# Attention outputs of one unit and scores of the next issued as one run of small matmuls, with masked scores and decayed keys and queries kept in the unit's own tile, and a new hand-written order for the first chunk

## Chip, cores and metric

The kernel runs on one core of one Trainium2 chip. Its time is the device time of one execution in microseconds (us); the figure that counts is the median over runs. The engines that matter are TensorE (PE; its weight loads are listed as PEld), VectorE (DVE), ScalarE (ACT), and the SyncE queue (SP), which issues nearly all DMA transfers. Each engine works through its own instructions in order; semaphores tie the engines together.

## The reference

Two layers, one after the other, in 32-bit floats, for 4 batches, 8 heads, 768 positions and a head width of 64. First an attention with decay, in blocks of 64 positions:

```python
for b in range(nb):                       # 12 blocks of 64 positions
    intra = (q_b @ k_b^T) * Dmask         # scores inside the block, masked by powers of lam
    intra = intra @ v_b
    inter = (q_b * lam_pow) @ kv_state    # what earlier blocks left
    out_b = intra + inter
    kv_state = lam_block * kv_state + (k_b * rev_pow)^T @ v_b
```

Its output, as 3072 tokens by 512 features, goes through a feed-forward layer: `h = x @ w_in` (512 by 2048), `g = softplus(h)`, `out = g @ w_out` (2048 by 512).

## The kernel before

The 768 positions are six **chunks** of 128 (two blocks of 64 each). A **unit** g is one chunk and one pair of heads: 24 units, four per chunk, `g // 4` being the chunk. A unit's inputs lie in one tile `att`: q and k with features on the partitions, k and v again with positions on the partitions.

The feed-forward layer runs in 96 **steps** s, 16 per chunk (one for each 128 columns of `w_in`). `mlp1(s)` (line 351) is 12 matmuls of 128x512 into a PSUM bank h; `chain_act`, `chain_hi`, `chain_lo` (lines 339 to 349) turn h into softplus values g, split into a high and a low part; `mlp2([s - 4])` (line 365) is 12 matmuls into four accumulators o. Both operands are split into high and low parts, hence three matmuls per product. The weights are converted and split on the chip, in groups of two, by `scale` and `round` (ACT), `shift`, `sign`, `add` (DVE), `hi` (ACT) and `lo` (DVE), lines 207 to 235; this goes on until about step 16.

The attention of units 4 to 23 is done by these functions:

- `k_decay` (line 262, ACT) and `q_decay` (line 268, DVE) write decayed copies kd and qd into tiles of their own, of tag b2.
- `mm_scores` (line 275) is one run of 64x64 matmuls: the scores into the x half and the state's increments into the y half of a tile w. That tile comes from `work` (tag t, one buffer of two PSUM banks).
- `mask_scores` (line 301, DVE) writes the masked scores into another b2 tile, and `update_states` (line 315, DVE) computes the next states from y with four instructions.
- `mm_out` (line 288) is a second run of 64x64 matmuls, from states, qd, values and masked scores, into a tile z, also from `work`. `x_high` (ACT) and `x_low` (DVE) then split z into the x that `mlp1` reads.

In the record, a 64x64 product is two matmul instructions, so `mm_scores` and `mm_out` show 64 instructions each.

Chunk 0 (units 0 to 3) uses 128-wide versions of the same (S, m, O, Q and so on). Steps 0 to 5 are an order written out by hand as a text (line 485): each entry names a function and its numbers, for example `mlp 1 2` for p = 2 of `mlp1(1)`. `warm n` issues n matmuls of zeros that nobody reads; 16 of them run before the text (line 151). From step 6 on a loop (line 509) emits the work. The scores of a unit stand behind `mlp2` of one step, and its outputs behind `mlp2` of the step two later:

```python
    scores_at.update({4 * n + 1 + NF: 2 * NP + n for n in range(NG - 2 * NP)})
    outs_at = {6: 4, **{s + 2: g for s, g in scores_at.items()}}
```

The PSUM banks are: o with four buffers (also used in chunk 0), h with two, and the two banks of `work`. A tile of a tag takes a bank whose earlier tile has been released at that place of the program, and its first writer waits until the last reader of that earlier tile is done. SBUF tiles of tag b8 (21 buffers) hold units, raw and split weights, x and the output rows.

Of the kernel before, what the change touches and what calls it, by code (L numbers as in the profile page):

```python
# [31 lines left out]
def decay_attention_softplus_ffn(  # L32
# [197 lines left out]
    def w_hi(*ks):  # L230
        nc.scalar.copy(out=w_at(ks)[:, 0], in_=conv[ks[0]].bitcast(F32))  # L231

    def w_lo(*ks):
        w = w_at(ks)
        nc.vector.tensor_sub(out=w[:, 1], in0=conv.pop(ks[0]).bitcast(F32), in1=w[:, 0])  # L235
# [38 lines left out]

    def mm_scores(g, x, y):
        q, k, kd, v = q_of(g), k_of(g), kds.pop(g), vt_of(g)
        for b in range(B):
            for t in range(2):
                cols = slice((2 * b + t) * 64, (2 * b + t + 1) * 64)
                for s in range(2):  # L280
                    r = half(s)
                    nc.tensor.matmul(x[r, cols], lhsT=k[r, b, t], rhs=q[r, b, t], start=True, stop=True)  # L282
                    if s == 0 or not last_chunk(g):
                        nc.tensor.matmul(  # L284
                            y[half(1 - s), cols], lhsT=kd[r, b, t], rhs=v[r, b, t], start=True, stop=True
                        )

    def mm_out(g, w):
        a, qd, v, st = aa.pop(g), qds.pop(g), vt_of(g), states[g]
        for b in range(B):  # L290
            cols = slice(b * 64, b * 64 + 64)
            for s in range(2):
                r = half(s)
                for t in range(2):
                    nc.tensor.matmul(w[half(t), s, cols], lhsT=st[r, b, t], rhs=qd[r, b, t], start=True, stop=False)  # L295
            for s in range(2):
                r = half(s)
                for t in range(2):
                    nc.tensor.matmul(w[half(t), s, cols], lhsT=v[r, b, t], rhs=a[r, b, t], start=False, stop=True)  # L299

    def mask_scores(g, x):
        a = aa[g] = t2([128, B, 2, 64], F32, f"a_{g}")
        m = mask[:, heads(g), :].rearrange("q (o t) i -> q o t i", o=1).broadcast_to([128, B, 2, T])
        nc.vector.tensor_mul(out=a, in0=x.rearrange("q (b t i) -> q b t i", b=B, t=2), in1=m)  # L304
# [85 lines left out]
    def scores_of(g):  # L390
        w = work(f"w{g}")
        mm_scores(g, w[:, 0], w[:, 1])
        mask_scores(g, w[:, 0])
        update_states(g, w[:, 1])
# [80 lines left out]
    step = {  # L475
        "S": scores0, "m": mask0_scores, "O": out0, "xh": x0_high, "xl": x0_low, "kd": k0_decay, "kda": k0_decay_act,
        "Q": sums0, "sc": states0, "kd1": k_decay, "qd": q_decay, "sc1": scores1,
        "m1": lambda g: mask_scores(g, z[g][:, 0]), "up": lambda g: update_states(g, z[g][:, 1]), "out1": out1,
        "xh1": lambda g: x_high(g, z[g]), "xl1": lambda g: x_low(g, z[g]),
        "scale": w_scale, "round": w_round, "shift": w_shift, "sign": w_sign,  # L480
        "add": w_add, "hi": w_hi, "lo": w_lo, "act": chain_act, "ghi": chain_hi, "glo": chain_lo,
# [1 line left out]
        "warm": keep_warm, "load": w_load, "unit": load_upto, "qk": loads["qk"], "v": loads["v"], "kt": loads["kt"],  # L483
    }
    for line in """
        S 0, m 0 0, scale 0, m 0 1, round 0, warm 6, S 1, shift 0, sign 0, add 0, scale 1, m 1 0, m 1 1,
        shift 1, warm 3, O 0, hi 0, lo 0, round 1, xh 0, sign 1, S 2, xl 0, scale 2, mlp 0 0, add 1, m 2 0,
        hi 1, O 1, load 4, xh 1, v 2, kt 0, m 2 1, shift 2, round 2, lo 1, xl 1, S 3, v 3, kda 2, mlp 1 0, m
        3 1, m 3 0, load 5, scale 3, shift 3, kda 0, round 3, mlp 1 1, O 2, O 3, xh 2, Q 0, sign 2, load 6,
        sign 3, xh 3, mlp 0 1, load 7, add 2, add 3, xl 2, mlp 0 2, xl 3, load 8, scale 4, kt 1, shift 4,  # L490
        scale 5, mlp 1 2, mlp 0 3, shift 5, hi 2, lo 2, hi 3, sign 5, round 5, round 4, mlp 1 3, mlp 2 0,
        load 9, act 0, scale 6 7, lo 3, sign 4, add 5, ghi 0, add 4, mlp 2 1, kda 1, hi 4, mlp 3 0, hi 5,
        round 6 7, mlp 3 1, shift 6 7, glo 0, kt 3, mlp 2 2, lo 4, act 1, mlp 3 2, load 10, lo 5, sign 6 7,
        unit 5, scale 8 9, kd 3, mlp 2 3, add 6 7, ghi 1, mlp 3 3, kd1 4, unit 6, mlp 4, Q 1, Q 2, sc1 4, hi
        6 7, load 11, Q 3, glo 1, shift 8 9, lo 6 7, qd 4, mlp 5, act 2, sc 1, ghi 2, load 12, sign 8 9, sc
        0, sc 3, glo 2, sc 2, load 13, load 14, round 8 9, m1 4, act 3, ghi 3, unit 7, mlp2 0, up 4, scale
        10 11, add 8 9, glo 3, hi 8 9, shift 10 11, mlp2 1, load 15, act 4, lo 8 9, load 16, ghi 4, round 10
        11, sign 10 11, glo 4, add 10 11
    """.replace("\n", " ").split(","):
# [4 lines left out]
    scores_at = {7: 5, 10: 6, 13: 7}
    scores_at.update({4 * n + 1 + NF: 2 * NP + n for n in range(NG - 2 * NP)})
    outs_at = {6: 4, **{s + 2: g for s, g in scores_at.items()}}
    for s in range(6, last + LAG):
        if s + 1 in scores_at:  # L510
            k_decay(scores_at[s + 1])
            q_decay(scores_at[s + 1])
# [4 lines left out]
        old, new = w_group(s - 1), w_group(s)
        if old:
            w_hi(*old)
        if new:  # L520
            w_scale(*new)
            w_round(*new)
        if old:
            w_lo(*old)
        if new:
            w_shift(*new)
            w_sign(*new)
            w_add(*new)
# [4 lines left out]
        if s in scores_at:  # L533
            scores_of(scores_at[s])
        if s in outs_at:
            g = outs_at[s]
            w = work(f"z{g}")
            mm_out(g, w)
            x_high(g, w)
            x_low(g, w)  # L540
        if s < last:
            mlp1(s)
        w_load(2 * s + 6)
        ahead = scores_at if s < 13 else outs_at
        if s in ahead:
            load_upto(ahead[s] + 2)
# [37 lines left out]
```

## Time and profile before

| | |
|---|---|
| median of 3 runs | 603.29 us (602.88 to 603.33) |
| profiled execution | 603.04 us |
| its span, first to last instruction | 601.3 us |
| instructions in the span | 11190 |
| matmul instructions of PE | 5017 |
| matmuls of `mlp1` and of `mlp2` | 1152 and 1152 |
| bytes read from and written to memory | 41.95 MB and 6.29 MB |

The profile is of one execution. In the list of instructions in order of time, the columns are start in us, duration in us, engine, line of the kernel, operation, tiles written and read, shapes, and the count of merged instructions; in square brackets stands the idle time of the engine before them and what ended it. The end of a matmul is modelled, so lengths of stretches of PE work are best taken from start to start. In the table of windows the columns are the window, its length, and busy time and instruction count of each engine, then the granted TensorE clock (1.00 is full speed), the share of the DMA engines and their rate.

### The profile page before, as it was taken

The numbers are of one execution on the slowest core, as the hardware profiler recorded it, in microseconds if no ns is written. First come the engines' busy times: TensorE is split into PE (matmuls) and PEld (weight loads), VectorE is DVE, ScalarE is ACT, GpSimd is POOL, SyncE is SP. The second block draws the span as 40 slices with busy tenths as digits, with TensorE's granted clock in tenths as the row PEclk, the third lists the DMA queues.
The fourth block names the chain that finished last, engine by engine and source line by source line (L and its number), as shares of the span: only waits on it lengthen the run. The fifth ranks groups of instructions, "written<-read, shape, count | busy, mean of one in ns | idle before, by whom it ended". The sixth has DMA issues, their size and how long they took to land.

```text
span 601.3 us, 11190 instructions
## 1 busy us (share of the span) xinstructions
PE 595.7 (99%) x5017; PEld 486.0 (81%) x5017; DVE 226.3 (38%) x337; ACT 211.4 (35%) x343; POOL 1.5 (0%) x9
## 2 busy tenths in 40 slices
PE   9999999999999999999999999999999999999997
PEld 6788888888888888888888888888888888888885
DVE  7999999623223133331332322312322121211011
ACT  5897867422322223222222232222322222222211
POOL 1000000000000000000000000000000000000000
PEclk9999999999999999999999999999999999999999
DMA  8997322223002206002023200220500200100001
GB/s 291 416 416 280 138 72 71 71 101 111 1 2 71 71 1 211 1 1 71 1 71 132 79 1 6 68 71 0 211 1 1 71 0 1 71 0 1 1 1 70
DMA packets 15743, 48.95 MB, mean 81 GB/s; under 512 B 1872, under 2 KB 1872, under 8 KB 15696
## 3 DMA queue, kind: packets, MB, share of 16 engines
q1 hardware_dynamic: 15408, 47.72, 21.8%
q8 instruction: 39, 0.64, 0.5%
q10 hardware_dynamic: 288, 0.52, 0.2%
q14 instruction: 8, 0.07, 0.0%
HBM read 41.95 MB, written 6.29 MB: 80 GB/s over the span
## 4 chain that ended last, share of the span: by engine, by line
PE 98%; DVE 1%; issue 0%; ACT 0%; DVEq 0%
PE h L360 45%; PE o L377 43%; PE w L282 3%; PE z L295 2%; PE z L299 2%; PE warm_ps L149 1%; PE w L284 1%; PE z L426 0%; PE x L410 0%; PE y L455 0%; DVE att L416 0%; DVE x L436 0%; DVE c L222 0%; ACT x L432 0%; DVE c L218 0%
## 5 line engine op out<-in xcount | busy, mean ns | idle before, releaser
L360 PE MATMUL h<-x,w 128*128 128x512 f32 x1152 | 282.8, 394 | 0.3 <-DVE x L436 0.3
L377 PE MATMUL o<-w,g 128*128 128x512 f32 x1152 | 275.9, 389 | 0.0
L377 PEld LDWEIGHTS o<-w,g 128*128 128x128 f32 x1152 | 216.3, 188 | 44.8
L360 PEld LDWEIGHTS h<-x,w 128*128 128x128 f32 x1152 | 212.9, 188 | 46.8 <-DVE x L436 1.2
L349 DVE TENSOR_TENSOR g<-l,g 128x512 fp32r<-128x512 f32 x96 | 66.4, 692 | 262.4 <-ACT g L345 262.3
L341 ACT ACTIVATE l<-h 128x512 f32<-128x512 f32 x96 | 57.2, 596 | 264.6 <-PE h L360 259.6
L345 ACT CAST g<-l 128x512 fp32r<-128x512 f32 x96 | 59.6, 621 | 2.9
L266 ACT ACTIVATE kd<-att,rp 128x256 f32<-128x256 f32 x40 | 18.2, 505 | 60.7 <-DMA att<-in_att 60.7
L309 DVE SCALAR_TENSOR_TENSOR st<-st,lam_c,w 64x256 f32<-64x256 f32 x72 | 31.7, 480 | 0.8
L271 DVE TENSOR_TENSOR qd<-att,lp 128x512 f32<-128x512 f32 x20 | 13.8, 689 | 34.7 <-DMA att<-in_att 34.7
L332 DVE TENSOR_TENSOR x<-z,x 128x512 fp32r<-128x512 f32 x20 | 13.8, 690 | 34.0 <-ACT x L325 34.0
L282 PEld LDWEIGHTS w<-att 64*64 64x64 f32 x640 | 20.4, 134 | 6.8 <-issue 6.0
L325 ACT CAST x<-z 128x512 fp32r<-128x512 f32 x20 | 11.7, 586 | 35.9 <-PE z L299 35.9
L282 PE MATMUL w<-att 64*64 64x64 f32 x640 | 23.1, 221 | 0.0
L284 PE MATMUL w<-att,kd 64*64 64x64 f32 x576 | 23.0, 221 | 0.0
L304 DVE TENSOR_TENSOR a<-w,mask 128x512 f32<-128x512 f32 x20 | 13.8, 690 | 24.3 <-PE w L284 18.3
L295 PEld LDWEIGHTS z<-qd,st 64*64 64x64 f32 x640 | 17.0, 134 | 7.0 <-issue 7.0
L295 PE MATMUL z<-qd,st 64*64 64x64 f32 x640 | 20.9, 224 | 0.0
L235 DVE TENSOR_TENSOR w<-c,w 128x1024 fp32r<-128x1024 f32 (+1 forms) x19 | 20.0, 1055 | 1.5 <-ACT w L231 1.5
L228 DVE CUSTOM_DVE_ANT_0 c<-raw,c 128x2048 uint16<-128x2048 uint16 (+1 forms) x19 | 19.9, 1056 | 1.5
L284 PEld LDWEIGHTS w<-att,kd 64*64 64x64 f32 x576 | 20.3, 134 | 0.0
L222 DVE SCALAR_TENSOR_TENSOR c<-raw,c 128x1024 uint32<-128x1024 uint32 (+1 forms) x19 | 20.0, 1055 | 0.4
(42 smaller groups left out, 182.4 us busy)
## 6 DMA issues: line engine op xcount, KB each, us to landing
att<-in_att SPq DMA_DIRECT2D x44, 512.0 KB, 5.1
raw<-in_wts SPq DMA_DIRECT2D x32, 512.0 KB, 8.5
out_dram<-ob SPq DMA_DIRECT2D x22, 256.0 KB, 2.6
att<-in_att SPq DMA_DIRECT2D x8, 256.0 KB, 8.3
out_dram<-ob ACTq DMA_DIRECT2D x2, 256.0 KB, 2.0
lam_b<-in_lam SPq DMA_DIRECT2D x1, 4.0 KB, 2.7
```

What stands on the lines that cost most here:

```text
L222: nc.vector.scalar_tensor_tensor(out=c, in0=raw_at(ks, 1), scalar=0x80000000, in1=c, op0=ALU.bitwise_and, op1=ALU.bitwise_or)
L228: nc.vector.tensor_add(out=c, in0=c, in1=raw_at(ks, 0))
L235: nc.vector.tensor_sub(out=w[:, 1], in0=conv.pop(ks[0]).bitcast(F32), in1=w[:, 0])
L282: nc.tensor.matmul(x[r, cols], lhsT=k[r, b, t], rhs=q[r, b, t], start=True, stop=True)
L284: nc.tensor.matmul(y[half(1 - s), cols], lhsT=kd[r, b, t], rhs=v[r, b, t], start=True, stop=True)
L295: nc.tensor.matmul(w[half(t), s, cols], lhsT=st[r, b, t], rhs=qd[r, b, t], start=True, stop=False)
L309: nc.vector.scalar_tensor_tensor(out=to[:, :, t], in0=of[:, :, t], scalar=lam_c[r, h : h + 1], in1=u[:, :, t], op0=ALU.mult, op1=ALU.add,)
L341: nc.scalar.activation(l_tiles[s], h_tiles.pop(s), AF.Softplus)
L345: nc.scalar.copy(out=g_tiles[s][:, 0, :], in_=l_tiles[s])
L349: nc.vector.tensor_sub(out=g[:, 1, :], in0=l_tiles.pop(s), in1=g[:, 0, :])
L360: nc.tensor.matmul(h_tiles[s], lhsT=w[:, i, cs], rhs=x[:, j, :], start=p == 0 and n == 0, stop=p == NP - 1 and n == 2,)
L377: nc.tensor.matmul(o_tiles[c][b], lhsT=g[:, i, b * 128 : (b + 1) * 128], rhs=w[:, j], start=f == 0 and n == 0, stop=f == NF - 1 and n == 2,)
```

## The change

**Tiles.** The tag b2 is gone. `k_decay` writes over k (position-major), `q_decay` over q, and `mask_scores` over k (feature-major), all in the unit's own tile. b8 gets a 22nd buffer. `mm_scores` and `mm_out` read from these places.

**Banks.** From unit 5 on, scores and increments go into two tiles of tag h, x and y, instead of a `work` tile. `mlp1`'s own h tiles take turns with them in the same two banks.

**Order in the loop.** An event every four steps holds `out1` (`mm_out`) of unit g - 1 and, right behind it, `sc1` (`mm_scores`) of unit g. One `mlp2` is pulled ahead from the following step to stand between them and `mlp1(s)`. The loop starts at step 17.

**The text.** It now reaches to step 16, with new places for most entries, and the order of the first loads is new. The decay of k of unit 2 moves from ACT (`kda`) to DVE (`kd`), and there are four `warm` matmuls in the text in place of nine.

```diff
-        return sb.tile(shape, dt, tag="b8", bufs=21, name=name)
+        return sb.tile(shape, dt, tag="b8", bufs=22, name=name)
...
-    for line in "w 1, qk 1, w 2, v 1, v 0, qk 2, w 3, qk 3, kt 2".split(","):
+    for line in "w 1, qk 1, w 2, v 0, qk 2, v 1, w 3, qk 3, v 2".split(","):
...
-            nc.scalar.activation(kd[:, :, t], kt_of(g)[:, :, t], AF.Copy, scale=rp1[:, h : h + 1])
+            nc.scalar.activation(kt_of(g)[:, :, t], kt_of(g)[:, :, t], AF.Copy, scale=rp1[:, h : h + 1])
...
+        q = q_of(g).rearrange("q b t i -> q b (t i)")
+        nc.vector.tensor_mul(out=q, in0=q, in1=w)
...
-        nc.vector.tensor_mul(out=a, in0=x.rearrange("q (b t i) -> q b t i", b=B, t=2), in1=m)
+        nc.vector.tensor_mul(out=k_of(g), in0=x.rearrange("q (b t i) -> q b t i", b=B, t=2), in1=m)
...
     def scores1(g):
-        z[g] = work(f"w{g}")
-        mm_scores(g, z[g][:, 0], z[g][:, 1])
+        if g == NP:
+            w = work(f"w{g}")
+            xy[g] = w[:, 0], w[:, 1]
+        else:
+            xy[g] = bank(f"x{g}"), bank(f"y{g}")
+        mm_scores(g, *xy[g])
...
+        S 0, m 0 1, scale 0, shift 0, sign 0, round 0, m 0 0, add 0, warm 3, S 1, scale 1, warm 1, O 0, m 1
+        0, hi 0, round 1, xh 0, shift 1, lo 0, sign 1, xl 0, kt 0, m 1 1, kt 1, v 3, round 2, S 2, scale 2,
+        load 4, add 1, m 2 0, mlp 0 0, hi 1, load 5, m 2 1, lo 1, O 1, S 3, xh 1, shift 2, load 6, load 7,
+        xl 1, kda 0, m 3 1, mlp 1 0, kda 1, m 3 0, sign 2, add 2, scale 3, mlp 1 1, load 8, O 2, xh 2, shift
+        3, xl 2, round 3, hi 2, load 9, O 3, sign 3, lo 2, unit 5, xh 3, kt 2, scale 4, load 10, Q 0, Q 1,
+        add 3, scale 5, shift 4, xl 3, hi 3, mlp 1 2, round 5, shift 5, mlp 0 1, sign 4, mlp 2 0, round 4,
+        scale 6 7, kt 3, mlp 0 2, mlp 2 1, mlp 0 3, act 0, sc 0, lo 3, ghi 0, unit 6, sign 5, add 4, shift 6
+        7, load 11, mlp 1 3, mlp 3 0, add 5, hi 4, hi 5, sign 6 7, mlp 3 1, round 6 7, glo 0, mlp 3 2, lo 5,
+        act 1, add 6 7, kd1 4, kd 2, mlp 2 2, ghi 1, mlp 3 3, hi 6 7, glo 1, mlp 2 3, load 12, act 2, mlp 4,
+        lo 4, Q 2, kd 3, scale 8 9, ghi 2, lo 6 7, shift 8 9, glo 2, sign 8 9, sc 1, sc1 4, Q 3, up 4, load
+        13, sc 2, act 3, mlp 5, sc 3, round 8 9, load 14, scale 10 11, add 8 9, ghi 3, shift 10 11, glo 3,
...
+        12 13, ghi 5, add 12 13, scale 14 15, qd 4, load 18, hi 12 13, mlp 6, glo 5, shift 14 15, mlp2 2,
+        mlp2 3, out1 4, load 19, lo 12 13, load 20, act 6, round 14 15, sign 14 15, load 21, ghi 6, load 22,
+        sc1 5, m1 5, add 14 15, load 23, mlp2 4, round 16 17, xh1 4, scale 18 19, scale 16 17, up 5, hi 14
...
+    events = {s: 2 * NP + (s - NF) // 4 for s in range(NF, last - NF + 1, 4)}
+    ahead = 17 - LAG
+    for s in range(17, last + LAG):
+        if events.get(s + 1, NG) < NG:
+            run("kd1", events[s + 1])
...
-        elif s - LAG < last - 1:
+        elif s - LAG < last - 1 and ahead != s - LAG:
             mlp2([s - LAG])
...
+        if s in events:
+            g = events[s]
+            run("out1", g - 1)
+            if g < NG:
+                run("sc1", g)
+            run("xh1", g - 1)
+            if g < NG:
+                run("m1", g)
+            if s % NF == 0:
+                run("xl1", g - 1)
+            if g < NG:
+                run("up", g)
+            if s % NF:
+                run("xl1", g - 1)
+            if g < NG:
+                run("qd", g)
+            ahead = s - LAG + 1
+            mlp2([ahead])
+            load_upto(g + 2)
         if s < last:
             mlp1(s)
```

More of the change, by code (lines that the diff above doesn't have):

```diff
@@ L48, in t8 @@
     def t8(shape, dt, name):
-        return sb.tile(shape, dt, tag="b8", bufs=21, name=name)
+        return sb.tile(shape, dt, tag="b8", bufs=22, name=name)
     def t4(shape, dt, name):
         return sb.tile(shape, dt, tag="b4", bufs=7, name=name)
-    def t2(shape, dt, name):
-        return sb.tile(shape, dt, tag="b2", bufs=4, name=name)
     def tl(shape, dt, name):
@@ L250, in x_of @@
         return x_tiles[c, p // 2][:, :, p % 2]
-    aa, kds, qds, states = {}, {}, {}, {}
+    states = {}
     lo, hi = half(0), half(1)
@@ L262, in k_decay @@
     def k_decay(g):
-        kd = kds[g] = t2([128, B, 2, 64], F32, f"kd_{g}")
         for t in range(2):
             h = heads(g).start + t
-            nc.scalar.activation(kd[:, :, t], kt_of(g)[:, :, t], AF.Copy, scale=rp1[:, h : h + 1])
+            nc.scalar.activation(kt_of(g)[:, :, t], kt_of(g)[:, :, t], AF.Copy, scale=rp1[:, h : h + 1])
     def q_decay(g):
-        qd = qds[g] = t2([128, B, 2, 64], F32, f"qd_{g}")
         w = lp[:, heads(g), :].rearrange("q (o t) i -> q o (t i)", o=1).broadcast_to([128, B, 2 * T])
-        nc.vector.tensor_mul(
-            out=qd.rearrange("q b t i -> q b (t i)"), in0=q_of(g).rearrange("q b t i -> q b (t i)"), in1=w
-        )
+        q = q_of(g).rearrange("q b t i -> q b (t i)")
+        nc.vector.tensor_mul(out=q, in0=q, in1=w)
     def mm_scores(g, x, y):
-        q, k, kd, v = q_of(g), k_of(g), kds.pop(g), vt_of(g)
+        q, k, kd, v = q_of(g), k_of(g), kt_of(g), vt_of(g)
         for b in range(B):
@@ L288, in mm_out @@
     def mm_out(g, w):
-        a, qd, v, st = aa.pop(g), qds.pop(g), vt_of(g), states[g]
+        a, qd, v, st = k_of(g), q_of(g), vt_of(g), states[g]
         for b in range(B):
@@ L388, in w_group @@
         return (2 * j, 2 * j + 1) if 2 * j < NW else ()
[L390 to L394, printed above, removed]
     def whole(p, kind):
@@ L465, in states0 @@
             )
+    xy = {}
     def scores1(g):
-        z[g] = work(f"w{g}")
-        mm_scores(g, z[g][:, 0], z[g][:, 1])
+        if g == NP:
[4 more added lines that the diff above has]
+        mm_scores(g, *xy[g])
     def out1(g):
@@ L485, in decay_attention_softplus_ffn @@
     for line in """
[L486 to L495, printed above, removed]
@@ L496, in decay_attention_softplus_ffn @@
-        0, sc 3, glo 2, sc 2, load 13, load 14, round 8 9, m1 4, act 3, ghi 3, unit 7, mlp2 0, up 4, scale
-        10 11, add 8 9, glo 3, hi 8 9, shift 10 11, mlp2 1, load 15, act 4, lo 8 9, load 16, ghi 4, round 10
-        11, sign 10 11, glo 4, add 10 11
+        S 0, m 0 1, scale 0, shift 0, sign 0, round 0, m 0 0, add 0, warm 3, S 1, scale 1, warm 1, O 0, m 1
+        0, hi 0, round 1, xh 0, shift 1, lo 0, sign 1, xl 0, kt 0, m 1 1, kt 1, v 3, round 2, S 2, scale 2,
+        load 4, add 1, m 2 0, mlp 0 0, hi 1, load 5, m 2 1, lo 1, O 1, S 3, xh 1, shift 2, load 6, load 7,
@@ new lines, in decay_attention_softplus_ffn @@
+        act 1, add 6 7, kd1 4, kd 2, mlp 2 2, ghi 1, mlp 3 3, hi 6 7, glo 1, mlp 2 3, load 12, act 2, mlp 4,
+        lo 4, Q 2, kd 3, scale 8 9, ghi 2, lo 6 7, shift 8 9, glo 2, sign 8 9, sc 1, sc1 4, Q 3, up 4, load
+        13, sc 2, act 3, mlp 5, sc 3, round 8 9, load 14, scale 10 11, add 8 9, ghi 3, shift 10 11, glo 3,
+        mlp2 0, load 15, hi 8 9, load 16, round 10 11, lo 8 9, sign 10 11, m1 4, act 4, mlp2 1, round 12 13,
+        load 17, ghi 4, add 10 11, scale 12 13, glo 4, shift 12 13, hi 10 11, kd1 5, lo 10 11, act 5, sign
@@ new lines, in decay_attention_softplus_ffn @@
+        12 13, ghi 5, add 12 13, scale 14 15, qd 4, load 18, hi 12 13, mlp 6, glo 5, shift 14 15, mlp2 2,
+        mlp2 3, out1 4, load 19, lo 12 13, load 20, act 6, round 14 15, sign 14 15, load 21, ghi 6, load 22,
+        sc1 5, m1 5, add 14 15, load 23, mlp2 4, round 16 17, xh1 4, scale 18 19, scale 16 17, up 5, hi 14
+        15, shift 18 19, lo 14 15, mlp 7, load 24, shift 16 17, mlp 8, load 25, unit 7, glo 6, scale 20 21,
+        sign 16 17, load 26, act 7, mlp2 5, round 18 19, kd1 6, load 27, add 16 17, hi 16 17, ghi 7, mlp 9,
@@ new lines, in decay_attention_softplus_ffn @@
+        qd 5, sign 18 19, lo 16 17, round 20 21, glo 7, add 18 19, unit 8, scale 24 25, load 28, load 29,
+        act 8, mlp2 6, xl1 4, ghi 8, glo 8, hi 18 19, out1 5, shift 20 21, act 9, lo 18 19, sc1 6, ghi 9,
+        round 22 23, kd1 7, scale 22 23, sign 20 21, mlp2 7, m1 6, add 20 21, mlp 10, shift 22 23, up 6,
+        load 30, hi 20 21, shift 24 25, glo 9, scale 28 29, mlp 11, act 10, lo 20 21, ghi 10, mlp2 8, round
+        24 25, unit 9, qd 6, glo 10, sign 22 23, act 11, ghi 11, xh1 5, add 22 23, hi 22 23, xl1 5, load 31,
@@ new lines, in decay_attention_softplus_ffn @@
+        glo 11, mlp 12, lo 22 23, sign 24 25, add 24 25, act 12, out1 6, sc1 7, m1 7, scale 26 27, shift 26
+        27, ghi 12, round 28 29, hi 24 25, glo 12, kd1 8, sign 26 27, lo 24 25, mlp2 9, xh1 6, shift 28 29,
+        mlp 13, load 32, round 26 27, act 13, add 26 27, scale 30 31, sign 28 29, hi 26 27, add 28 29, lo 26
+        27, xl1 6, mlp2 10, mlp 14, hi 28 29, ghi 13, glo 13, round 30 31, mlp2 11, shift 30 31, act 14, qd
+        7, ghi 14, glo 14, up 7, mlp 15, lo 28 29, act 15, sign 30 31, out1 7, ghi 15, sc1 8, up 8, add 30
@@ L499, in decay_attention_softplus_ffn @@
+        31, mlp2 12, mlp2 13, m1 8, xh1 7, unit 10, xl1 7, hi 30 31, mlp 16, lo 30 31, qd 8, glo 15
     """.replace("\n", " ").split(","):
@@ L501, in decay_attention_softplus_ffn, with run @@
         step[name](*map(int, numbers))
+    def run(name, *numbers):
+        step[name](*numbers)
     last = NCH * NF
[L506 to L512, printed above, removed]
+    events = {s: 2 * NP + (s - NF) // 4 for s in range(NF, last - NF + 1, 4)}
[3 more added lines that the diff above has]
+            run("kd1", events[s + 1])
         if s - 1 < last:
@@ L516, in decay_attention_softplus_ffn @@
             chain_lo(s - 1)
[L517 to L528, printed above, removed]
         if s == last + LAG - 2:
             mlp2([s - LAG, s - LAG + 1])
-        elif s - LAG < last - 1:
+        elif s - LAG < last - 1 and ahead != s - LAG:
             mlp2([s - LAG])
[L533 to L540, printed above, removed]
+        if s in events:
[17 more added lines that the diff above has]
+            load_upto(g + 2)
         if s < last:
             mlp1(s)
[L543 to L546, printed above, removed]
 def _layout(q, k, v, lam, w_in, w_out):
```

3 lines of the change are left out of this document (1 added, 2 removed).

## The prediction, made before the changed kernel had run

> **What bounds the kernel now.** I read the page's busy line first, then the slices of DVE, then the chain of work that ended last.
>
> ```profile
> PE 595.7 (99%) x5017; PEld 486.0 (81%) x5017; DVE 226.3 (38%) x337; ACT 211.4 (35%) x343; POOL 1.5 (0%) x9
> DVE  7999999623223133331332322312322121211011
> PE 98%; DVE 1%; issue 0%; ACT 0%; DVEq 0%
> ```
>
> TensorE is busy for 99% of the span and makes 98% of the chain, so only what shortens TensorE's own queue can shorten the kernel. The second row has a warning: from the second to the seventh of 40 slices (15 to 105 us, while weights are converted) VectorE is at 90% or more, so there a shorter TensorE queue helps only as far as VectorE keeps up.
>
> How TensorE spends its time is seen in the list in order of time, from start to start:
>
> ```profile
> 54.93 0.27 PE L282 MATMUL w<-att 64*64 64x64 f32 x1
> ...
> 56.02 3.02 PE L360 MATMUL h<-x,w 128*128 128x512 f32 x12
> 58.88 2.88 PE L377 MATMUL o<-w,g 128*128 128x512 f32 x12
> 61.60 2.88 PE L360 MATMUL h<-x,w 128*128 128x512 f32 x12
> 64.32 2.88 PE L377 MATMUL o<-w,g 128*128 128x512 f32 x12
> 67.13 0.34 PE L295 MATMUL z<-qd,st 64*64 64x64 f32 x8
> ...
> 67.41 0.30 PE L295 MATMUL z<-qd,st 64*64 64x64 f32 x8
> ...
> 67.88 0.30 PE L295 MATMUL z<-qd,st 64*64 64x64 f32 x8
> ...
> 68.22 3.02 PE L360 MATMUL h<-x,w 128*128 128x512 f32 x12
> 71.08 2.88 PE L377 MATMUL o<-w,g 128*128 128x512 f32 x12
> ```
>
> Twelve large matmuls in the middle of a stretch take 61.60 - 58.88 = 2.72 us, 0.227 each. The outputs of a unit start 67.13 - 64.32 = 2.81 after the twelve before them (0.09 late), run for 68.22 - 67.13 = 1.09, and the twelve behind them take 71.08 - 68.22 = 2.86 (0.14 late). One run of 64 small instructions thus costs 0.09 + 1.09 + 0.14 = 1.32 us. Inside it, 32 instructions pass in 67.88 - 67.41 = 0.47, so 64 take 0.94 of pure work. The rest, 1.32 - 0.94 = **0.38 us, is the price of going into small matmuls and out again**. The scores' run has the same figures: 56.02 - 54.93 = 1.09, then 2.86.
>
> **The change, part by part.**
>
> *The joined runs.* Units 4 to 23 have 20 runs of scores and 20 of outputs. Afterwards the outputs of units 4 to 22 stand right in front of the scores of units 5 to 23, with nothing for TensorE between them, in the text as in the loop: 19 entries and exits go. The number of small and large matmuls stays. Is the seam between the two free? Two places of chunk 0 bear on it:
>
> ```profile
> 16.06 1.09 PE L426 MATMUL z<-att 128*64 128x128 f32 x16
> 17.08 1.16 PE L410 MATMUL x<-att 64*128 64x128 f32 x16
> ...
> 19.77 1.97 PE L426 MATMUL z<-att 128*64 128x128 f32 x32
> 21.57 0.64 PE L455 MATMUL y<-att 128*64 128x64 f32 x16
> ...
> 34.27 1.15 PE L455 MATMUL y<-att 128*64 128x64 f32 x32
> 35.36 0.27 PE L282 MATMUL w<-att 64*64 64x64 f32 x1
> ...
> 36.45 0.69 PE L455 MATMUL y<-att 128*64 128x64 f32 x16
> 37.06 3.02 PE L360 MATMUL h<-x,w 128*128 128x512 f32 x12
> ```
>
> Outputs of one unit of chunk 0 before another form take 17.08 - 16.06 = 1.02; two such runs of the same form back to back take 21.57 - 19.77 = 1.80 rather than 2.04, so joining them did save 0.24 here. Where the form changes (128*64 to 64*64 and back), the scores between take 36.45 - 35.36 = 1.09, as beside large matmuls: of the 0.38, the 0.15 inside the run stays. So a join saves between 0.38 - 0.15 = 0.23 (the seam acts as a change of form) and 0.38 (it acts as the same form). Scores and outputs both are 64*64, and inside a run operands and banks alternate without a gap; I take 0.38. **19 x 0.38 = 7.2 us**; the low end is 19 x 0.23 = 4.4.
>
> The Trainium skill, TensorEngine Tiling (Array Packing), Key Properties, says that changing the tiling mode drains TensorE, while changing the tile within a mode does not. By that rule the seam is free and the sum stays at 7.2; by the row of the changed form it would be 4.4. No run here has shown this very seam yet.
>
> *New waits around the joined run.* Scores of unit g now write the two h banks, so they wait for `chain_act(s-1)` to have read the last h, and `mlp1(s)` waits for the mask to have read x. A quiet event of the old loop prices both:
>
> ```profile
> 118.34 3.02 PE L360 MATMUL h<-x,w 128*128 128x512 f32 x12
> 118.48 0.69 DVE L304 TENSOR_TENSOR a<-w,mask 128x512 f32<-128x512 f32 x1 [1.86 <-PE w L284]
> 119.18 1.79 DVE L309 SCALAR_TENSOR_TENSOR st<-st,lam_c,w 64x256 f32<-64x256 f32 x4
> ...
> 121.40 0.60 ACT L341 ACTIVATE l<-h 128x512 f32<-128x512 f32 x1 [5.51 <-PE h L360]
> ```
>
> The softplus read starts 0.20 after the twelve matmuls' successors begin (118.34 + 2.86 = 121.20) and ends at 0.80; by then TensorE is in `mlp2(s-4)` with 2.81 of it and 0.94 of outputs before the scores, 3.75 in all: 2.9 us to spare. The mask ends 119.17 - 118.34 = 0.83 after the small run, and `mlp2(s-3)`, pulled ahead for this, covers 2.86: 2.0 to spare. Behind a waiting `mlp1` would stand all of TensorE's queue, so without that cover each late microsecond would count. Should `mlp1(s)` get y's bank, it waits for the four state updates (120.97, 2.63 after): still 0.2 to spare, except in the four events at multiples of 16, where `x_low` (0.69, as the mask) goes first: 0.5 late each. The step behind an event has two `mlp1` in a row; the updates are done before the second. The moved `mlp2` needs g of s - 3, three steps old. Outputs at s = 32, 48, 64 and 80 feed `mlp1(s)` at once: ACT's split, the mask and `x_low` end about 0.83 + 0.69 after the run, under the same 2.86. All this I cost at nothing.
>
> *Values in the unit's own tile, b8 22.* k is overwritten by the mask after the matmuls that read it, q by `q_decay` behind the updates, k position-major by ACT a step ahead. No instruction is added, and each of these writers already waited for the same matmuls or has TensorE's large blocks beside it. A unit's load is issued four steps before its use, behind the outputs that free its slot; the page's list of DMA issues gives its landing:
>
> ```profile
> att<-in_att SPq DMA_DIRECT2D x44, 512.0 KB, 5.1
> ```
>
> Four steps are over 4 x 2 x 2.72 = 21.8 us, so 5.1 is hidden. Nothing.
>
> *The first chunk.* Here the bound is closer:
>
> ```profile
> L349 DVE TENSOR_TENSOR g<-l,g 128x512 fp32r<-128x512 f32 x96 | 66.4, 692 | 262.4 <-ACT g L345 262.3
> 22.13:39.92 17.79, 17.71 (x180) 14.37 (x176) 17.71 (x28) 17.65 (x34) 0.00 (x0) 1.00 1.03 418
> 61.60:80.56 18.96, 18.96 (x202) 15.41 (x200) 18.12 (x23) 14.22 (x19) 0.00 (x0) 1.00 0.24 87
> 34.26 0.69 DVE L218 TENSOR_SCALAR c<-c 128x1024 uint32<-128x1024 uint32 x1
> 34.87 1.23 DVE L235 TENSOR_TENSOR w<-c,w 128x1024 fp32r<-128x1024 f32 x1
> 62.05 1.22 DVE L235 TENSOR_TENSOR w<-c,w 128x1024 fp32r<-128x1024 f32 x1
> ```
>
> Of 25 matmuls of zeros (16, 6 and 3 in the code) 20 stay: 5 x 0.227 = 1.1 us less for TensorE, if it has something to do instead. From 22.13 to 39.92 (first window: TensorE, weight loads, VectorE, ScalarE) VectorE works 17.71 of 17.79 us. `mlp1(5)` needs `lo 6 7`, which ends at 34.87 + 1.23 = 36.10; it starts at 37.06, so TensorE can come at most 0.96 earlier before it waits for VectorE. Counted through both texts, VectorE has 44 entries up to `lo 6 7` in each, the same ones but for `kd 2` in place of `shift 8 9` (a 128x512 product takes 0.69 in the first row, a shift 0.69 at 34.26): no earlier, no later. **I take 0.9 of the 1.1.** The ends: 1.1, and minus 1.2, if the new order puts one conversion of 1.23 ahead of what TensorE waits for.
>
> The loads are the same transfers in another order. At 418 GB/s a transfer of 512 KB takes 1.25 us and one of 256 KB 0.63. v of unit 0 goes before v of unit 1 (0.63 earlier for `O 0`); the fourth raw weight falls behind three quarter tiles and comes 3 x 0.63 = 1.9 later; ACT's `scale 3` and what is queued behind it (`xh 2` first) wait for it, and VectorE's `shift 3` after those, while TensorE has `mlp 1 1` and two chunk-0 outputs ahead of the first user, `mlp 3 0`. If that cover is gone, it counts within the minus 1.2. SP issues them; the transfers of SP that come later in the text move with it, and 418 GB/s is all that the stretch takes in either order.
>
> *Steps 6 to 16.* Four of the joins lie here, 4 x 0.38 = 1.5 us. Three steps take 18.96 us with 18.12 of VectorE (second window); with a join they take 18.58, still more than VectorE's. The tightest place is `lo 14 15`, done at 62.05 + 1.22 = 63.27 for matmuls at 64.32, 1.05 to spare. TensorE would come 0.9 + 0.4 = 1.3 earlier. But up to this entry the new text has 1.2 less for VectorE (`qd 5`, `xl1 4`, `glo 6`, `glo 7` come later; `kd 2` and a `shift` come earlier): two entries of 0.6 to 0.7, so about 0.9 stays. I take nothing off.
>
> *Sum.* 7.2 + 0.9 = 8.1 us off the profiled execution's 603.04 (span 601.3 and 1.7 around it): 594.9. The median shown is 0.25 above that execution, so **595.2 us**.
>
> **The rivals.**
>
> *VectorE takes over in steps 0 to 16.* For it: the 90% slices, and margins of about 1 us. Against: 44 entries against 44, and the entries put off. It gives back the 0.9 and the four joins, 2.4: 597.6.
>
> *The seam is a drain.* The joins don't do what the change says: 4.4 + 0.9 = 5.3, so 598.0. For it: the row of the changed form; against: one form on both sides.
>
> *TensorE's clock falls.* The windows show the clock granted in full (1.00) with zeros filling the first waits; fewer zeros may let it idle. At half the clock each twelve matmuls cost 2.72 more, so one such block gives 597.9. Against it: the waits that I find in a walk through the text are under 1 us. The Trainium skill, TensorE: Matmul & The Clock Gate, part 1, says that an idle window of about 3.4 us halves the clock; no window of this trace shows it.
>
> *Slower: the shared h banks become TensorE's wait.* One mechanism: at each of 19 joined runs `mlp1(s)`, or the scores, stands until VectorE or ScalarE has emptied a bank. Up to 0.38 + 0.9/19 = 0.43 us per run this only eats the gain; from there on the kernel is slower, and at 0.6 it would take 595.2 + 11.4 = 606.6. For it: in steps 6 to 16 VectorE reaches the mask behind conversions of 1.2 us each. Against: 2.0 us to spare in the quiet part, where 15 of the 19 lie.
>
> **How the numbers follow.** Forecast (594.0 to 596.4): 0.68. VectorE takes over (596.4 to 598): 0.15. Seam: 0.07. Clock: 0.02. Bank waits that eat the gain: 0.04 about even, 0.04 slower. The range reaches from 594.0 (all of the zeros and 0.3 more) to 598.3, which takes in the low end of the seam. A measurement of this kernel can tell some 0.2% (1.2 us) from no change; so faster 0.92, same 0.04, slower 0.04.
>
> **What the profile afterwards would show.** Right: 19 runs of 128 small instructions, about 2.03 us from start to start, with 0.09 and 0.14 around them; in the quiet part no idle time of TensorE, and each event 0.38 shorter than two old runs; `mlp1(5)` near 36.2. Wrong: a gap of 0.15 in the middle of a joined run (seam); TensorE's idle time put down to DVE lines 218 to 235 or to the mask (VectorE, banks); a granted clock under 1.00 in the first 40 us. The whole falls if a joined run costs 2 x 1.32 as before.

## The result, and the profile after

| | before | after |
|---|---|---|
| median | 603.23 us (602.88 to 603.33) | 599.30 us (597.80 to 599.66) |
| profiled execution | 603.04 us | 599.38 us |
| its span | 601.3 us | 597.6 us |

The ratio is 0.9931 with a 95% interval of 0.9914 to 0.9949: faster by 3.9 us where 8.1 were forecast, and outside the range. The lines of the changed kernel are other ones than those printed above: L353 is `mlp1`, L370 `mlp2`, L289 and L293 the outputs, L276 and L278 the scores and increments, L297 the mask, L396 the scores of chunk 0, L412 its outputs, L418 and L422 their splits `xh` and `xl`, L431 the decays of its k (`kda`), L441 its sums (`Q`), L207 `scale`, L215 `shift`, L219 `sign`, L225 `add`, L232 `lo`.

Of the page after, the busy line, the granted clock in 40 slices, and the chain:

```profile
PE 589.6 (99%) x5012; PEld 486.5 (81%) x5012; DVE 224.8 (38%) x338; ACT 209.9 (35%) x341; POOL 1.5 (0%) x9
PEclk9899999999999999999999999999999999999999
PE 96%; DMA 3%; SPq 0%; DVE 0%; ACT 0%; issue 0%
```

TensorE is still busy for 99%, but two things are new, both early: transfers make 3% of the chain, and the second slice (15 to 30 us) has a clock of less than 0.9. The first is not the loss: the kernels of experiments 1 and 4, which win the time back, show the same share of transfers. The second is part of the loss.

An event of the quiet part, in order of time, shows the joined run:

```profile
133.72 2.88 PE L370 MATMUL o<-w,g 128*128 128x512 f32 x12
136.54 0.34 PE L289 MATMUL z<-att,st 64*64 64x64 f32 x8
...
138.56 3.02 PE L370 MATMUL o<-w,g 128*128 128x512 f32 x12
141.42 2.88 PE L353 MATMUL h<-x,w 128*128 128x512 f32 x12
```

128 small instructions run from 136.54 to 138.56, 2.02 us where two runs took 2 x 1.09. The twelve before them take 2.82 and those behind 2.86, once per event instead of twice. Nothing waits. This run is one of the four shortest; the other 15 of the 19 take 2.04 to 2.06, and the twelve behind them 2.85 to 2.90. What all the joins are worth is seen between two marks that stand in both kernels, the start of `mlp1(5)` and that of the last 48 matmuls: before 37.06 (in the prediction) and the first row here, after the other two.

```profile
586.41 11.04 PE L377 MATMUL o<-w,g 128*128 128x512 f32 x48
```

```profile
40.06 1.19 PE L353 MATMUL h<-x,w 128*128 128x512 f32 x4
...
582.76 1.52 PE L370 MATMUL o<-w,g 128*128 128x512 f32 x6
```

586.41 - 37.06 = 549.35 and 582.76 - 40.06 = 542.70: 6.65 us less for 19 joins, **0.35 each**. But `mlp1(5)` starts 3.0 us **later** than before, where the prediction had it 0.9 earlier. The list in order of time shows what happened:

```profile
19.05 1.09 PE L412 MATMUL z<-att 128*64 128x128 f32 x16
...
20.51 0.67 ACT L207 ACTIVATE c<-raw 128x512 f32<-128x512 f32 x1 [1.80 <-DMA raw<-in_wts]
21.08 0.57 ACT L418 CAST x<-z 128x512 fp32r<-128x512 f32 x1
21.22 0.43 DVE L215 TENSOR_SCALAR c<-c 128x512 uint32<-128x512 uint32 x1
...
21.69 0.69 DVE L422 TENSOR_TENSOR x<-z,x 128x512 fp32r<-128x512 f32 x1
...
22.43 1.09 PE L412 MATMUL z<-att 128*64 128x128 f32 x16 [2.29 <-DVE x L422]
```

Read from below: `O 3` (22.43) waits 2.29 us for `xl 2` (21.69); that waits for `xh 2` (21.08), which stands on ACT behind `scale 3` (20.51), which waited 1.80 us for the fourth raw weight, now loaded later. In the old text `O 3` stood ahead of `xh 2` and `xl 2`. The table of windows shows the second loss:

```profile
19.05:23.36 4.31, 2.02 (x34) 1.78 (x34) 4.10 (x8) 2.21 (x4) 0.00 (x0) 1.00 1.02 414
23.36:26.00 2.64, 2.64 (x39) 2.33 (x36) 2.06 (x5) 2.42 (x5) 0.00 (x0) 0.57 1.03 421
26.00:30.00 4.00, 4.00 (x17) 3.20 (x16) 4.00 (x8) 2.00 (x3) 0.00 (x0) 0.85 1.04 418
```

Behind the stretch in which TensorE worked 2.02 of 4.31 us, the granted clock is 0.57 and then 0.85: 2.64 x 0.43 + 4.00 x 0.15 = 1.7 us of its speed are lost. The two losses make 4.0, and the start is 3.0 later. The 1.0 between them is a remainder, what the new start gains otherwise; 0.7 of it is there already at `O 2`, which starts at 19.05 and stood at 19.77 before. In one of the four executions the clock stayed at 1.000; that is the one of 597.80.

### The profile page after: what moved, and what is told of

It is laid out like the page before. It is cut to its first block, busy times and chain, and to the rows that moved or that the text cites. A ratio compares the mean times of both kernels' runs of the same rounds, so it can differ in the third digit from the quotient of the medians.

```text
span 597.6 us, 11198 instructions
## 1 busy us (share of the span) xinstructions
PE 589.6 (99%) x5012; PEld 486.5 (81%) x5012; DVE 224.8 (38%) x338; ACT 209.9 (35%) x341; POOL 1.5 (0%) x9
## 4 chain that ended last, share of the span: by engine, by line
PE 96%; DMA 3%; SPq 0%; DVE 0%; ACT 0%; issue 0%
PE o L370 45%; PE h L353 44%; PE x L276 2%; PE z L289 2%; PE z L293 2%; DMA att<-in_att 1%; DMA raw<-in_wts 1%; PE y L278 1%; PE y L441 0%; PE z L412 0%; PE w L276 0%; SPq L124 0%; SPq L83 0%; SPq L86 0%; DVE x L422 0%; DVE ob L376 0%
## 5 line engine op out<-in xcount | busy, mean ns | idle before, releaser
L370 PE MATMUL o<-w,g 128*128 128x512 f32 x1152 | 278.8, 392 | 0.0
L353 PE MATMUL h<-x,w 128*128 128x512 f32 x1152 | 275.2, 391 | 0.3 <-DVE x L422 0.3
L353 PEld LDWEIGHTS h<-x,w 128*128 128x128 f32 x1152 | 216.7, 188 | 46.3 <-DVE x L422 0.9
L370 PEld LDWEIGHTS o<-w,g 128*128 128x128 f32 x1152 | 214.7, 188 | 45.6
L302 DVE SCALAR_TENSOR_TENSOR st<-st,lam_c,y 64x256 f32<-64x256 f32 x68 | 29.9, 480 | 2.4 <-PE y L278 1.3
L297 DVE TENSOR_TENSOR att<-x,mask 128x512 f32<-128x512 f32 x19 | 13.1, 691 | 43.5 <-PE y L278 24.0
L289 PEld LDWEIGHTS z<-att,st 64*64 64x64 f32 x640 | 17.0, 134 | 7.0 <-issue 6.3
L276 PE MATMUL x<-att 64*64 64x64 f32 x608 | 21.4, 218 | 0.0
L278 PE MATMUL y<-att 64*64 64x64 f32 x544 | 21.2, 219 | 0.0
L289 PE MATMUL z<-att,st 64*64 64x64 f32 x640 | 20.9, 224 | 0.0
L225 DVE CUSTOM_DVE_ANT_0 c<-raw,c 128x2048 uint16<-128x2048 uint16 (+1 forms) x19 | 20.0, 1052 | 0.6 <-ACT raw L211 0.4
L232 DVE TENSOR_TENSOR w<-c,w 128x1024 fp32r<-128x1024 f32 (+1 forms) x19 | 20.0, 1051 | 0.4 <-ACT w L228 0.3
L219 DVE SCALAR_TENSOR_TENSOR c<-raw,c 128x1024 uint32<-128x1024 uint32 (+1 forms) x19 | 19.9, 1049 | 0.0
L207 ACT ACTIVATE c<-raw 128x1024 f32<-128x1024 f32 (+1 forms) x19 | 18.7, 996 | 3.4 <-DMA raw<-in_wts 3.4
L293 PE MATMUL z<-att 64*64 64x64 f32 x640 | 19.9, 218 | 0.0
L276 PEld LDWEIGHTS x<-att 64*64 64x64 f32 x608 | 19.8, 135 | 0.0
L278 PEld LDWEIGHTS y<-att 64*64 64x64 f32 x544 | 19.6, 135 | 0.0
L228 ACT CAST w<-c 128x1024 fp32r<-128x1024 f32 (+1 forms) x19 | 17.2, 913 | 6.4 <-DVE c L225 6.4
```

The costliest lines, as they stand in the source:

```text
L225: nc.vector.tensor_add(out=c, in0=c, in1=raw_at(ks, 0))
L278: nc.tensor.matmul(y[half(1 - s), cols], lhsT=kd[r, b, t], rhs=v[r, b, t], start=True, stop=True)
L302: nc.vector.scalar_tensor_tensor(out=to[:, :, t], in0=of[:, :, t], scalar=lam_c[r, h : h + 1], in1=u[:, :, t], op0=ALU.mult, op1=ALU.add,)
L353: nc.tensor.matmul(h_tiles[s], lhsT=w[:, i, cs], rhs=x[:, j, :], start=p == 0 and n == 0, stop=p == NP - 1 and n == 2,)
L370: nc.tensor.matmul(o_tiles[c][b], lhsT=g[:, i, b * 128 : (b + 1) * 128], rhs=w[:, j], start=f == 0 and n == 0, stop=f == NF - 1 and n == 2,)
```

## The experiments

The theory after the two traces: the joins work as meant, and the shortfall sits in the new order of chunk 0, where `O 3` was put behind `xl 2`. Ten kernels tested it, each timed beside the kernel before (its median was 603.0 to 603.1 in these sets).

**1. `O 3` moved ahead.**

```diff
-O 2, xh 2, shift 3, xl 2, round 3, hi 2, load 9, O 3, sign 3,
+O 2, O 3, xh 2, shift 3, xl 2, round 3, hi 2, load 9, sign 3,
```

> Edit: the entry O 3 stands right behind O 2, ahead of xh 2, shift 3 and xl 2; nothing else. Theory A (the 2.3 us in front of O 3 are only there because O 3 shares the tile z with xl 2, and the clock falls because of that idle time): O 3 follows O 2 without a gap, the two sums behind it too, and TensorE waits less than 1 us at mlp 1 2 for xl 2, which stays where it was (done near 22.4 us). Start of mlp1(5) from 40.1 to about 37 us, clock 1.00 throughout, time about 596.3. Theory B (the late weight holds TensorE wherever the entries stand): the wait of 2.3 us only moves to mlp 1 2, the clock still falls, time 599.0 to 599.6.

Measured: 596.08 us, ratio 0.9887 (0.9872 to 0.9901), clock 1.000 in all executions.

```profile
19.10 1.97 PE L412 MATMUL z<-att 128*64 128x128 f32 x32
20.89 1.10 PE L441 MATMUL y<-att 128*64 128x64 f32 x32
21.93 1.30 PE L353 MATMUL h<-x,w 128*128 128x512 f32 x4
```

```profile
20.55 0.70 ACT L207 ACTIVATE c<-raw 128x512 f32<-128x512 f32 x1 [1.90 <-DMA raw<-in_wts]
```

The weight comes as late as before (ACT waits 1.90 us for it), but now TensorE has the outputs and the two sums to do meanwhile and goes on without a gap. `mlp1(5)` starts at 36.56. Theory A holds; 3.2 us come back from one entry of the text.

**2. The late weight loaded earlier.**

```diff
-... xl 0, kt 0, m 1 1, kt 1, v 3, round 2, S 2, scale 2, load 4, add 1,
+... xl 0, load 4, kt 0, m 1 1, kt 1, v 3, round 2, S 2, scale 2, add 1,
```

> Edit: the load of the fourth raw weight stands ahead of kt 0, kt 1 and v 3 instead of behind them; nothing else. Theory A (the root is that weight's landing at 20.5 us, which holds ScalarE's scale 3 and xh 2 behind it, then VectorE's shift 3 and xl 2, then O 3): it lands near 17.9, scale 3 no longer waits for it, and O 3 starts between 20.3 and 20.9 instead of 22.4; the clock stays at 1.00; time 595.5 to 596.5. Theory B (v 3 and the two kt tiles, now about 1.2 us later each, take its place as the wait): O 3 waits for v 3 until 19.5 only, but the sums Q 0 and Q 1 wait for the decays, and the time falls by less than 1 us, to 598.5 or more.

Measured: 598.60 us (597.40 to 600.95), ratio 0.9931 (0.9913 to 0.9948). A miss for A; the time is B's, but not the wait that B named.

```profile
18.13 1.71 ACT L431 ACTIVATE att<-att,rp 128x256 f32<-128x256 f32 x4 [1.22 <-DMA att<-in_att]
19.74 0.67 ACT L207 ACTIVATE c<-raw 128x512 f32<-128x512 f32 x1
20.31 0.57 ACT L418 CAST x<-z 128x512 fp32r<-128x512 f32 x1
```

```profile
21.99 1.09 PE L412 MATMUL z<-att 128*64 128x128 f32 x16 [1.93 <-DVE x L422]
```

Now ACT waits 1.22 us for kt of unit 0 in front of the decays (L431), and `scale 3` and `xh 2`, queued behind, start only 0.77 earlier than in the changed kernel. `O 3` still waits 1.93 us for `xl 2`. In a queue that works in order, one late transfer took the place of the other; the landing of that weight was not the root. In three of the six executions the clock fell (0.994 to 0.997, 599.6 to 601.0 us; the others 597.4 to 597.6). Where it didn't fall, the edit brings some 0.2 to 0.4 us (the changed kernel's one such execution took 597.80), as the wait is shorter by 0.36. The profiled execution is one of those.

**3. Zeros in the gap.**

```diff
-... hi 2, load 9, O 3, sign 3,
+... hi 2, load 9, warm 10, O 3, sign 3,
```

> Edit: ten matmuls of zeros (2.3 us) in front of O 3, where TensorE idles; the wait itself stays. Theory A (1.7 us of the loss is the halved clock that follows the idle time): clock 1.00 throughout in every run, O 3 at 22.4 to 22.7 us, mlp1(5) at about 38.5, time 597.6 to 597.9, like the one run of the changed kernel whose clock did not fall (597.8). Theory C (the clock falls for another reason, or its fall costs nothing because VectorE sets the pace there): time stays at 599.2 to 599.6, or the clock shows 0.997 again.

Measured: 598.07 us, ratio 0.9919 (0.9906 to 0.9932), clock 1.000 in all executions; `O 3` at 22.82, `mlp1(5)` at 38.88.

```profile
22.82:30.00 7.18, 7.18 (x72) 6.23 (x72) 6.00 (x11) 5.22 (x9) 0.00 (x0) 1.00 1.03 414
```

The wait is kept, its 2.3 us are filled, and 1.2 us come back, 1.6 if the 0.4 by which the zeros delay `O 3` is added. That prices the clock apart from the wait: A, a little above its figure. Start to start, the way from the sums (`Q 0`) to `mlp1(5)` agrees: 40.06 - 23.36 = 16.70 us in the changed kernel, 38.88 - 23.74 = 15.14 here, 1.56 less. In experiment 1 that way takes 36.56 - 20.89 = 15.67: some 0.5 us is lost there in short waits, the longest near 31 us for a `lo` on VectorE that is done at 31.47, so that half of the 1.0 that the new start gains is left.

**4. A bank of its own for unit 3's outputs, text as changed.**

```diff
+        if p == 3:
+            z3[3] = obank("z3")
...
+                    z_at(p)[half(t), b * C : (b + 1) * C], lhsT=v[:, b, t], rhs=a[:, t, b],
```

> Edit: the changed kernel with its text untouched, so O 3 stands behind xl 2, but unit 3's chunk-0 outputs go into a PSUM bank of their own (tag o) instead of the second bank of the tile z that xl 2 reads. Theory A (O 3 waits because it shares a tile with xl 2, although it writes the other bank): O 3 follows O 2 without the wait of 2.3 us, clock 1.00, time 595.8 to 596.6 as with O 3 moved. Theory E (something else that stands between O 2 and O 3 in the text holds it, a load or the place in the queues): the wait stays at 2 us and the time at 598 to 599.7.

Measured: 595.80 us, ratio 0.9879 (0.9866 to 0.9893), clock 1.000; the 32 instructions of both units follow each other from 18.33 to 20.12, and `mlp1(5)` starts at 36.68. `O 3` needed nothing that `xl 2` makes. It waited because both use the tile z, though in different banks. A place behind a reader of the same tile is a wait, and a second tile takes it away as well as another place.

**5. The joins of the loop undone** (on the kernel of experiment 1).

```diff
         elif s - LAG < last - 1 and ahead != s - LAG:
+            if s in events:
+                run("out1", events[s] - 1)
             mlp2([s - LAG])
         if s in events:
             g = events[s]
-            run("out1", g - 1)
```

> Edit: the kernel with O 3 moved, and in the loop the outputs of unit g - 1 stand in front of the mlp2 that runs between them and the scores of unit g: the 15 joins of the loop (from step 20 on) are undone, nothing else moves. Theory A (each join is worth 0.35 us, by leaving out one way into the small matmuls and out again): 596.1 + 15 x 0.35 = 601.3, and each event longer by 0.35. Theory F (the joins are worth less, and the gain comes from elsewhere, say from fewer waits): below 599.

Measured: 601.28 us, ratio 0.9968 (0.9956 to 0.9980). 601.28 - 596.08 = 5.2 us for 15 joins, 0.35 each.

**6. The joins with the old start and the old order of steps 0 to 15.** The old text and first loads; the old loop from step 6 with its weight conversions, and the events (shown against the changed kernel):

```diff
+    events = {7: 5, 10: 6, 13: 7}
+    events.update({s: 2 * NP + (s - NF) // 4 for s in range(NF, last - NF + 1, 4)})
...
+    for s in range(6, last + LAG):
...
+        if new:
+            w_shift(*new)
+            w_sign(*new)
+            w_add(*new)
...
```

> Edit: the joined runs, values in the unit's tile, 22 buffers and shared h banks of the changed kernel, but the old text, old first loads and old loop for steps 0 to 15 (with the joined events at steps 7, 10, 13 and 16): the joins without the new order of chunk 0. Theory A (the joins are worth 0.35 us each wherever they stand, and all of the shortfall sits in the new start): no idle time and clock 1.00 in the first 40 us, mlp1(5) at 37.1 as in the kernel before, 603.2 - 19 x 0.35 = 596.6. Theory D (in steps 6 to 16 VectorE in its old order cannot keep up with the earlier TensorE, so the new order is needed for the joins): idle time of TensorE put down to VectorE between 40 and 115 us, time 598 or more.

Measured: 604.56 us, ratio 1.0024 (1.0015 to 1.0033): slower than before, and theory A misses by 8 us. The start costs nothing (`mlp1(5)` at 36.47, expected at 37.1). The waits and the list around step 7 show the place:

```profile
PE h L353 <- DVE att L297: 3.1, 3, 1.0
PE o L370 <- DVE w L232: 2.4, 5, 0.6
```

```profile
55.21 0.69 DVE L215 TENSOR_SCALAR c<-c 128x1024 uint32<-128x1024 uint32 x1
55.93 1.22 DVE L219 SCALAR_TENSOR_TENSOR c<-raw,c 128x1024 uint32<-128x1024 uint32 x1
57.29 1.23 DVE L225 CUSTOM_DVE_ANT_0 c<-raw,c 128x2048 uint16<-128x2048 uint16 x1
58.43 0.68 DVE L297 TENSOR_TENSOR att<-x,mask 128x512 f32<-128x512 f32 x1
```

```profile
59.17 1.19 PE L353 MATMUL h<-x,w 128*128 128x512 f32 x4 [1.02 <-DVE att L297]
```

```profile
68.39:89.93 21.54, 19.60 (x202) 15.16 (x200) 18.39 (x23) 14.00 (x19) 0.00 (x0) 1.00 0.27 98
```

The joined run ended near 55.0, but the mask stands behind three entries of a conversion and comes at 58.43; `mlp1`, whose bank it frees, waits 1.02 us. The window holds three steps with one join: 21.54 us where 18.96 (the prediction's second window) less 0.35 was to be had, with VectorE at work for 18.39 us, 18.12 before. Three such stretches in a row take 63.98 us instead of 55.83, and that is the whole of the 8 us; the listed waits add up to less, since the modelled ends of the matmuls hide a part of each. This is the prediction's slower rival, in the steps where conversions run, with the old order.

**7. The same with the mask first.** In the event steps `w_shift`, `w_sign` and `w_add` move behind the updates:

```diff
-        if new:
+        if new and s not in events:
             w_shift(*new)
...
             if g < NG:
                 run("up", g)
+            if new:
+                w_shift(*new)
...
```

> Edit: the kernel of old start and old order with joined runs at steps 7, 10, 13 and 16 (604.6), but in these steps VectorE's shift, sign and add of the new weight group stand behind the mask and the state updates instead of ahead of them. Theory D1 (VectorE has the time, and the loss is its order: the mask that frees the bank for mlp1 stands behind 3.1 us of conversions): the waits of TensorE for the mask (3 of 1.0 to 1.5 us) go, and with them part of the waits for lo in the step behind; 599 to 601.5. Theory D2 (VectorE is simply full in these steps, whatever its order): the waits move from the mask to lo, and the time stays within 0.6 us of 604.6.

Measured: 600.55 us, ratio 0.9960 (0.9948 to 0.9973). The waits for the mask are gone; those for `lo` (2.4 us) stay. 4.0 of the 8 us come back by order alone, so D1 for that half. The other half, the waits for `lo`, was not tried by itself. The new text does the same conversions by 113.8 us (experiment 1) with neither wait, so an order that avoids both exists; which of its moves avoids the second isn't shown.

**8. The events from step 16 on only,** separate runs before that (old text, old order):

```diff
+        if s in scores_at:
+            for name in ("sc1", "m1", "up", "qd"):
+                run(name, scores_at[s])
...
+        if s in outs_at:
+            for name in ("out1", "xh1", "xl1"):
+                run(name, outs_at[s])
```

> Edit: the old text, old first loads and the old order of steps 0 to 15 with separate runs (units 5 to 7 in a work tile), and the events of the changed kernel only from step 16 on, 16 joins. Theory A (the joins cost nothing else once the weights are converted; the loss of the second order was VectorE's in steps 6 to 15): 603.1 - 16 x 0.35 = 597.5, no idle time of TensorE after 120 us. Theory G (the shared h banks or the mlp2 pulled ahead make TensorE wait in the quiet part too): idle time of TensorE put down to the mask or the updates at the events, time 599 or more.

Measured: 597.86 us, ratio 0.9913 (0.9900 to 0.9927). 16 joins bring 5.3 us, 0.33 each. Once the weights are converted, the shared banks and the `mlp2` pulled ahead cost nothing; without any new order of chunk 0 the loop alone brings no less than the whole change. Its median is 1.4 us lower, but the intervals overlap, and the changed kernel's one execution with a full clock (597.80) lies among its times.

**9. Fewer zeros in the kernel before.**

```diff
-        S 0, m 0 0, scale 0, m 0 1, round 0, warm 6, S 1, ... shift 1, warm 3, O 0,
+        S 0, m 0 0, scale 0, m 0 1, round 0, warm 3, S 1, ... shift 1, warm 1, O 0,
```

> Edit: the kernel before, with 3 and 1 matmuls of zeros in the text instead of 6 and 3; nothing else of the change. The prediction's step (five zeros fewer give TensorE 1.1 us of which 0.9 can be used, since VectorE is done with lo 6 7 0.96 us before mlp1(5)): mlp1(5) at about 36.2 instead of 37.1, and since no join follows the rest keeps that lead, 602.2 to 602.4. Rival (the zeros only filled waits for VectorE and for loads, so TensorE waits in their place): mlp1(5) at 36.9 to 37.1, 602.9 to 603.2, or, if the clock falls for it, above 603.3.

Measured: 603.12 us, ratio 1.0002 (0.9993 to 1.0011), `mlp1(5)` at 36.95. The rival holds. TensorE's waits in their place (L426 are the outputs of chunk 0 in this kernel, L410 its scores):

```profile
PE z L426 <- DMA att<-in_att: 1.4, 2, 0.9
PE x L410 <- DMA att<-in_att: 0.8, 2, 0.5
```

2.2 us of waits for loads: the zeros had filled time in which the data were not there. 1.1 us of them stand for the five zeros; the rest is there because the first scores start 1.0 us earlier in this profile (6.84 for 7.84; see the last section), and that gain too ends in front of the loads.

**10. 13 zeros at the start instead of 16** (on the kernel of experiment 1; `keep_warm(13)`).

> Edit: the kernel with O 3 moved, and 13 instead of 16 matmuls of zeros before the first scores. A try for a better version. Theory A (VectorE sets the pace of the first 36 us, and it idles about 1 us in front of the first mask for scores that stand behind the zeros, while their data have landed at 6.8): first scores about 0.7 earlier, mlp1(5) 0.3 to 0.7 earlier, 595.4 to 595.8, clock 1.00. Rival (the clock is not yet raised or falls again with fewer zeros): granted clock under 1.00 or first matmuls of the scores slower, 596.1 or more.

Measured: 595.87 us (595.43 to 596.37), ratio 0.9881 (0.9867 to 0.9894), clock 0.999 to 1.000; `mlp1(5)` at 36.14. The start is 0.4 earlier in the profiled execution, but the times lie across those of experiment 1: no gain that these runs can tell. The best kernels of the study are experiments 1, 4 and 10, at 595.8 to 596.1 us, 3.2 to 3.5 us below the changed kernel and 7.0 to 7.3 below the one before. That lies within the range that was forecast for the changed kernel.

## Why the prediction was wrong, step by step

- **The price of a run of small matmuls: right in its mechanism, 0.03 too high.** 0.38 per join was forecast, 0.35 measured (6.65 / 19; 0.35 when undone in experiment 5). The sum's term was 7.2 and came out as 6.65. The seam acts as the same form, up to some 0.03: 15 of the 19 joined runs took 2.04 to 2.06 us rather than the 2.03 worked out. By the rule of the Trainium skill, TensorEngine Tiling (Array Packing), Key Properties, it is free, and the trace agrees up to that.
- **The first chunk: wrong, 3.9 us of the 4.4 that are missing from the span.** The step that failed is "I take 0.9 of the 1.1" with a low end of minus 1.2. It looked at what VectorE must do before `mlp1(5)` and at how much later the weight comes, and took `mlp 3 0` for the first user on TensorE, with the two chunk-0 outputs ahead of it as cover. One of these two, `O 3`, was itself the user. The prediction didn't ask which entries `O 3` had been moved past. `xh 2` and `xl 2` read the tile that `O 3` writes, so the new place made a wait, which handed the late weight through ACT and VectorE to TensorE: 2.3 us. Experiments 1 and 4 each take it away, by place and by tile. The start came 3.0 us later instead of 0.9 earlier: this wait and the clock that fell after it, less what the new start gains. The signs of being wrong named the conversions on VectorE (lines 218 to 235) and the mask; the line that TensorE waited for, `xl 2`, is neither.
- **The clock: the rival at 0.02 came true as a consequence.** It was tied to fewer zeros; the cause was the 2.3 us gap (filled with zeros, the clock stayed at 1.000 in all four executions of experiment 3), and its price 1.2 to 1.6 us (the same experiment), 1.7 by the windows, where the rival had 2.7. The Trainium skill, TensorE: Matmul & The Clock Gate, part 1, puts the limit near an idle window of 3.4 us. Here 2.3 us idle, with TensorE at work for 2.02 of 4.31, was enough in three of four executions; the measurement decides.
- **The zeros: the 0.9 was no term of its own.** Alone in the old kernel they bring nothing (experiment 9), because VectorE was not the only bound: the loads were late too. The 0.5 that experiment 1's start gains (36.56 for 37.06, in two profiles whose first scores start within 0.1 us) comes with the new order as a whole.
- **Steps 6 to 16, "I take nothing off": right in its result, by too little working.** The joins there hold, but a margin of 1.05 us at one place and a sum of VectorE's time did not show it. With the old order VectorE's rows add up to much the same and the kernel loses 8 us (experiment 6). Where the mask stands in its queue decides half of it (experiment 7); the waits for `lo` are gone with the new text as a whole, and which move does it stays open. A new order was needed there, and the new text did harm only at `O 3`.
- **The covers in the quiet part: right.** No wait of TensorE at any event from step 16 on, in experiment 8 too.
- **The range: its lower end doesn't add up.** "All of the zeros and 0.3 more" is 0.2 + 0.3 below 595.2, 594.7 and not 594.0. The measured time lies beyond the other end.

## What to carry to other kernels

When an entry of a hand-written order moves, list every reader and writer of its tiles that it is moved past, not only the data it needs: two banks of one tile still wait for each other, and the wait passes on whatever stands in those engines' queues. A sum of an engine's work and a margin at one place don't show whether it keeps up; walk its queue to the entry that frees a buffer. Matmuls of zeros are worth what is ready to take their place, and a gap that they could have filled may cost the clock on top.

## What was not expected of the hardware

- About 2.3 us without work on TensorE was enough to halve its granted clock: it is 0.50 from 23.75 to 27.17 us of the profile after, and fell in three of four executions of that kernel. In experiment 2 it fell in three of six; the wait of 1.9 us is that of a profile in which it did not fall. The same program thus has times 1.4 to 3.6 us apart.
- The fall lasts 3.41 us, and the clock records of all twelve traces fit a grid of that size: from one change of the clock to the next there is always a whole multiple of 3.41 us. In the profile after, the clock rose to full at 6.69 and fell at 23.75, five times 3.41 later. The stretch of the grid before the fall held 2.1 us of the gap (20.34 to 22.43); in experiment 2's profile such a stretch held 1.8 us of the gap, and the clock stayed. So it may depend on how the gap lies in the grid whether one execution is hit; a single trace with a fall doesn't show it.
- The zeros at the start run at 0.43 us each and then at 0.23; the change came between 4.5 and 7.0 us after the span's start, so that the first scores, which stand behind the 16 zeros, start anywhere between 6.83 (experiment 4) and 7.88 us (experiment 3). The windows show a clock of 1.00 even while the zeros take 0.43 us, so a clock of 1.00 there says nothing. `mlp1(5)` follows in part at most: with the old text it starts at 36.47 and 36.95 (experiments 6 and 9, first scores at 6.84), and at 37.06 in the kernel before (7.84).
